# A table loaded in two transfers instead of four, thirteen matmuls ahead of a small network, two constants set by another engine

## The chip, the cores and the metric

The kernel runs on one core of a Trainium2 chip. The metric is the device time of one execution in microseconds (us), as the median over several runs; lower is better. Beside the timed runs there is one profiled execution, whose trace is quoted below.

## The reference, cut to what matters

Attention over 4 batches, 8 heads, 576 positions and 64 dimensions, with a bias that a small network makes from the distance of two positions; then a mixing step of low rank and a two-layer MLP over the 512-wide result.

```python
scores = scale * np.matmul(q, k.transpose(0, 1, 3, 2))
psi_rel = np.log1p(np.abs(pos[:, None] - pos[None, :]))
psi_i = np.log1p(np.maximum(pos[:, None], 1.0))
h = np.maximum((psi_rel / psi_i)[..., None] @ w1 + b1, 0.0)    # 32 hidden units
scores = scores + (h @ w2).transpose(2, 0, 1)[None]
attn = np.exp(scores - scores.max(-1)) / (sum + 1e-09)
x = heads of np.matmul(attn, v), side by side
u = x + (x.transpose(0, 2, 1) @ U @ V).transpose(0, 2, 1)
out = u + np.maximum(u @ w_ch1, 0.0) @ w_ch2
```

## The kernel before

The program is one long list per engine, written out by hand; each engine runs its list in order and waits at semaphores. SyncE (SP) and ScalarE (ACT) issue the DMAs, each on a queue of its own. The kernel has three stages: the bias network (about the first 65 us), the 16 pairs of heads of the attention, and the MLP. The change touches only the start of the first.

**The network.** Positions go in 36 groups of 16 rows (T = 32 to 35 first, then 0 to 31). For each T there are four hidden tiles (cg = 0 to 3), each 128 partitions (4 rows of positions times 32 hidden units) by up to 576 distances: `relu(table + psi)`, where the table is log1p of the distance times w1 and psi is one number per partition. `bias_hid` (L299) makes them: cg 0 by ACT (L308), cg 1 to 3 by VectorE (DVE, L310). `bias_mm` (L320) multiplies them by w2 on TensorE (PE, L328): the four cg use four column groups of 32 and run beside each other. `bias_out` (L339) scales the result from PSUM into SBUF by ACT (L342), and SP stores it to DRAM (L345), from where it is loaded again, row by row shifted, as the bias of the scores. ACT alternates between L308 of a later T and L342 of an earlier one. Between them stand the first steps of the attention: ACT casts q and k of the first pair (`raw`) into `hi` (L182) and DVE takes the difference (L192).

**What comes before the network.** `head` in DRAM is 128 x 641: column 0 is w1, and columns 1 on are the table for four subs of 32 rows each, of which sub s is read from column 1 + s on. Four loads fetch it into `tab` (L284), two issued by SP (subs 0, 1) and two by ACT (subs 2, 3). SP then issues w1 (L285, 128 rows of 4 bytes), `ident` (L781) and the two halves of `raw` (L154); ACT issues `small` (L286: b1, psi, w2 and scales, 128 rows of 852 bytes), then loads its function table and runs a first `warm` instruction (L289). DVE multiplies the table by w1 (L293), then psi by b1 (L294), then sets two constants (L782 `sgn`, L783 `eps`), and starts on the hidden tiles. GpSimd (POOL) clears two strips at the start (L276, L278) and has nothing else to do until L798.

Of the kernel before, what the change touches and what calls it, by code (L numbers as in the profile page):

```python
# [9 lines left out]
F32 = mybir.dt.float32  # L10
# [9 lines left out]
B, H, S, D = 4, 8, 576, 64  # L20
HP = H // 2
DM = H * D
# [3 lines left out]
HID = 32  # L26
P = 128
# [5 lines left out]
LINE = 16  # L33
NTAB = 2 * S - 1
CUT = 640
# [10 lines left out]
ALL_DVE = (6, 12, 16, 19, 24)  # L46

CW = 256

KD = DM // P  # L50
WQ = KD * DM
# [10 lines left out]
def kernel(  # L62
# [14 lines left out]
    nc = tc.nc  # L77
    mm = nc.tensor.matmul
# [14 lines left out]
    def psum(tag, shape, name):  # L93
        rot[tag].append(rot[tag].pop(0))
        pl = rot[tag][-1]
        return pl.tile(shape, F32, tag="a" if pl is psA else tag, name=name)
# [22 lines left out]
    sgn = const.tile([P, 1], I32, name="sgn")  # L119

    eps = const.tile([P, 9], F32, name="eps")[:, 0:1]
# [4 lines left out]
    x_sb = mix.tile([P, 5, DM], F32, name="x_sb")  # L126
# [24 lines left out]
    def load_part(p, a, e):  # L151
        b, hp = divmod(p, HP)
        for lo in (0, D):
            nc.sync.dma_start(out=raw[lo : lo + D, a:e], in_=qk[b, hp, :, a:e])  # L154
# [76 lines left out]
    def conv_ops(src, n, finish):  # L231
        st = {}

        def load():
            st["raw"] = wrawp.tile([P, CW], I64, tag="wraw", name="wraw")
            nc.sync.dma_start(out=st["raw"][:, 0:n], in_=src)
            words = st["raw"].bitcast(I32).rearrange("p (n t) -> p n t", t=2)
            st["l"], st["h"] = words[:, 0:n, 0], words[:, 0:n, 1]

        def size():  # L240
            st["t"] = wcp.tile([P, CW], I32, tag="t", name="wt")[:, 0:n]
            st["y"] = wyp.tile([P, CW], I32, tag="wy", name="wy")[:, 0:n]
            nc.scalar.activation(out=st["t"].bitcast(F32), in_=st["h"].bitcast(F32), func=AF.Abs)
# [32 lines left out]
    nc.gpsimd.memset(e5[:, NE:], 0.0)  # L276
    e_all = ring[1][:, 3 * S : 3 * S + 5 * (S + LINE)].rearrange("p (i y) -> p i y", i=5)
    nc.gpsimd.memset(e_all[:, :, NE : S + LINE], 0.0)  # L278
    e_ring = [e_all[:, i, :] for i in range(5)] + [e5]
    w1_sb, tab = wtab[:, S : S + 1], wtab[:, 0:S]  # L280
    small_sb = tabp.tile([P, SMALL], F32, name="small_sb")
    for sub in range(4):
        rows = slice(sub * HID, (sub + 1) * HID)
        (nc.sync, nc.scalar)[sub // 2].dma_start(out=tab[rows], in_=head[rows, 1 + sub : 1 + sub + S])  # L284
    nc.sync.dma_start(out=w1_sb, in_=head[:, 0:1])  # L285
    nc.scalar.dma_start(out=small_sb, in_=small)  # L286
    warm = tabp.tile([P, 1], F32, name="warm")
    nc.vector.memset(warm, 0.0)
    nc.scalar.activation(out=warm, in_=warm, func=AF.Relu)  # L289

    b1_sb, psi_sb = small_sb[:, 0:1], small_sb[:, 1 : 1 + S // 4]
# [466 lines left out]
    def weight_jobs(g, fin):  # L758
        jobs = []
        for which in range(2):  # L760
            for k in range(KD):
                for a in range(0, DM, CW):
                    if which == 0:
                        src = w_ch1[k * P : (k + 1) * P, g * DM + a : g * DM + a + CW]
                    else:
                        r = (g * FG + k) * P
                        src = w_ch2[r : r + P, a : a + CW]
                    jobs.append((src, CW, fin(g, which, k, a, a + CW)))
# [10 lines left out]

    pools["pt"] = p1.enter_context(tc.tile_pool(name="ptp", bufs=1, side="left"))  # L780
    nc.sync.dma_start(out=ident, in_=ident_in)  # L781
    nc.vector.memset(sgn.bitcast(F32), -2.0)  # L782
    nc.vector.memset(eps, 1.0e-9)  # L783
    load_part(0, 0, QKW)
    new_pair(0)
    order = [32, 33, 34, 35] + list(range(32))
# [5 lines left out]
    for i in range(len(order) + 2):  # L792
# [4 lines left out]
        if i == len(order) - 1:  # L797
            nc.gpsimd.tensor_scalar(  # L798
                out=warm, in0=hids[order[i]][3][:, 0:1], scalar1=1.0, scalar2=0.0, op0=ALU.mult, op1=ALU.add
# [24 lines left out]
    for c, hp in ((4, 1), (3, 0), (0, 1)):  # L824
# [6 lines left out]
        out=rep[:, 0 : 3 * RANK].rearrange("p (g r) -> p g r", g=3),  # L831
# [5 lines left out]
        out=rep[:, 3 * RANK : P], in0=fold[:, 0:RANK], in1=fold[:, 0:RANK], op=ALU.subtract  # L837
# [28 lines left out]
    for p in range(NP):  # L866
# [6 lines left out]
        for s in range(9):  # L873
# [27 lines left out]
            if p == NP - 3 and s == 1:  # L901
                t = big.tile([P, 9 * S], F32R, tag="big0", name="w1q")
# [3 lines left out]
            if p == NP - 2 and s == 1:  # L906
                t = big.tile([P, 9 * S], F32R, tag="big1", name="w2q")
# [5 lines left out]
            if p == NP - 1 and s == 1:  # L913
                t = big.tile([P, 9 * S], F32, tag="big2", name="acc")
# [65 lines left out]
    t = big.tile([P, 9 * S], F32R, tag="big3", name="ut")  # L980
    h1, h3, l3 = big_views(t, [(2 * UT, KD)] * 2 + [(UT, 2)])
    utq = t
    t = [qkp.tile([P, K0 + 2 * LINE], F32R, tag="lo", name="ut") for _ in range(2)]
# [67 lines left out]
    def turns(j):  # L1051
        return [lambda a=a, i=i: make_ut(a, i) for a in (j, j + 1) for i in range(TT)] if j < NB else [lambda: None] * 4
# [158 lines left out]
    t = turns(3)  # L1211
# [173 lines left out]
    for q in range(NQ):  # L1385
# [6 lines left out]
        segs, c = layer1(q)  # L1392
# [3 lines left out]
        first, pend = pend[:2], pend[2:]  # L1396
# [12 lines left out]
    for n, q in enumerate(order2):  # L1409
# [4 lines left out]
        one, c = layer1(q)  # L1414
# [84 lines left out]
```

## Time and profile before

| | |
|---|---|
| time, median of 3 runs | 729.49 us (728.93 to 730.12) |
| time of the profiled execution | 727.51 us |
| its span, first to last instruction | 725.7 us |
| TensorE busy in the span | 707.5 us (97%) |
| VectorE, ScalarE, GpSimd busy | 537.1, 402.9, 273.1 us |
| DMA traffic | 127.19 MB, mean 175 GB/s |
| granted TensorE clock, mean | 1.000 |

The span runs from the first to the last instruction; the profiled execution's own time is 1.8 us more than its span. It is 2.0 us under the median of the three timed runs, so a change in time is worked out against the profiled execution and then put on the median. Busy time of TensorE counts pipelined matmuls that overlap; at the start of the program TensorE waits for data, and how long is read from the first microseconds of the trace.

### The profile page before, as it was taken

Reading aid. Unit: us, or ns where it says so; the run is one execution under the profiler, and the core shown is the slowest. Engines: PE = TensorE matmul, PEld = TensorE weight load, DVE = VectorE, ACT = ScalarE, POOL = GpSimd, SP = SyncE. Lnnn points to the kernel's source line nnn. Section 1 sums busy time; section 2 is a strip of 40 time slices with the busy share of each in tenths; the row PEclk is TensorE's granted clock in tenths of the full one; section 3 lists DMA queues with packets and bytes.
Section 4 is the critical chain, followed back from the end, with each engine's and each line's share of the span. In section 5 each row is a group of like instructions: output and inputs, shape, how many; then the busy total and the mean of one; then the engine's idle time right before and its main releaser. Section 6 shows DMA issues by size and latency. Waiting matters only on the chain.

```text
span 725.7 us, 13129 instructions
## 1 busy us (share of the span) xinstructions
PE 707.5 (97%) x4620; PEld 561.2 (77%) x4620; DVE 537.1 (74%) x1202; ACT 402.9 (56%) x915; POOL 273.1 (38%) x287
## 2 busy tenths in 40 slices
PE   6999999999999999999999999999999999999997
PEld 2547888788777877878787888888787788888886
DVE  7985688788787777656658689999999953655545
ACT  7897778788778778864223335555555421222220
POOL 0006967567655557701150323536436300000000
PEclk9999999999999999999999999999999999999999
DMA  6889984565565546522293504637434665633313
GB/s 204 272 312 294 304 230 117 140 184 159 140 176 156 144 122 183 182 97 88 74 355 128 206 29 153 217 135 275 149 117 160 239 259 180 256 125 122 155 58 117
DMA packets 53393, 127.19 MB, mean 175 GB/s; under 512 B 8784, under 2 KB 12368, under 8 KB 52048
## 3 DMA queue, kind: packets, MB, share of 16 engines
q1 hardware_dynamic: 53088, 126.10, 53.1%
q8 instruction: 37, 0.61, 0.4%
q10 hardware_dynamic: 240, 0.26, 0.1%
q14 instruction: 28, 0.23, 0.1%
HBM read 81.34 MB, written 44.99 MB: 174 GB/s over the span
## 4 chain that ended last, share of the span: by engine, by line
PE 74%; ACT 9%; DVE 9%; issue 3%; DMA 2%; POOL 2%; SPq 0%; DVEq 0%; POOLq 0%; ACTq 0%
PE po L1334 15%; PE sb L1273 12%; PE o L508 11%; PE sc L399 10%; PE ph L676 7%; PE tb L472 7%; PE po L701 5%; PE bs L328 2%; ACT p L425 1%; POOL wy L266 1%; DVE acc L1320 1%; ACT pt L452 1%; ACT ring L308 1%; PE ph L1362 1%; ACT ring L342 1%
## 5 line engine op out<-in xcount | busy, mean ns | idle before, releaser
L1320 DVE TENSOR_TENSOR acc<-po,acc 128x512 f32<-128x512 f32 x108 | 74.1, 687 | 50.5 <-PE po L1334 44.1
L425 ACT ACTIVATE p<-p,st 128x576 f32<-128x576 f32 x128 | 99.9, 781 | 11.0 <-DVE st L407 10.6
L407 DVE CUSTOM_DVE_ANT_0 p<-sc,bias 128x576 f32<-128x576 f32 x128 | 95.9, 751 | 9.2 <-DMA bias<-bias_dram 4.7
L266 POOL TENSOR_TENSOR wy<-wt,wy 128x256 int32<-128x256 int32 (+1 forms) x68 | 50.3, 740 | 135.4 <-DVE wt L261 118.4
L399 PE MATMUL sc<-hi 128*128 128x288 f32 x320 | 100.6, 331 | 0.1
L399 PE MATMUL sc<-lo,hi 128*128 128x288 f32 x320 | 89.1, 295 | 0.0
L508 PE MATMUL o<-pt,v 128*64 128x320 f32 (+1 forms) x640 | 85.4, 411 | 0.1
L472 PE MATMUL tb<-ident,p 128*128 128x128 f32 x512 | 78.3, 275 | 1.4 <-DVE pt L454 0.9
L1334 PE MATMUL po<-wq,hq 128*128 128x512 f32 x288 | 73.5, 391 | 0.5 <-DVE ut L1367 0.5
L399 PEld LDWEIGHTS sc<-hi 128*128 128x128 f32 x320 | 60.3, 189 | 11.5 <-issue 8.0
L472 PEld LDWEIGHTS tb<-ident,p 128*128 128x128 f32 x512 | 59.8, 140 | 10.9 <-issue 7.6
L508 PEld LDWEIGHTS o<-pt,v 128*64 128x64 f32 x640 | 44.4, 136 | 30.1 <-issue 3.0
L452 ACT COPY pt<-tb 128x512 f32<-128x512 f32 x88 | 51.3, 582 | 23.4 <-PE tb L472 23.2
L1334 PEld LDWEIGHTS po<-wq,hq 128*128 128x128 f32 x288 | 53.5, 188 | 12.6 <-DVE ut L1367 0.9
L399 PEld LDWEIGHTS sc<-lo,hi 128*128 128x128 f32 x320 | 60.6, 189 | 0.5
L1273 PE MATMUL sb<-ut,w1q 128*128 128x512 f32 x216 | 55.1, 390 | 0.4 <-ACT acc L1277 0.3
L1273 PE MATMUL sb<-ut,wq 128*128 128x512 f32 x216 | 55.0, 390 | 0.5 <-ACT acc L1277 0.4
L328 PE MATMUL bs<-ring,small_sb 128*32 128x512 f32 (+48 forms) x640 | 43.8, 400 | 9.2 <-ACT ring L308 6.7
L701 PE MATMUL po<-w2q,hh 128*128 128x512 f32 x216 | 52.2, 393 | 0.4 <-DVE x_sb L576 0.4
L1334 PE MATMUL po<-w2q,ut 128*128 128x512 f32 x180 | 49.1, 389 | 0.0
L676 PE MATMUL ph<-ut,w1q 128*128 128x512 f32 (+1 forms) x240 | 48.2, 351 | 0.5 <-DVE ut L646 0.5
L1277 ACT COPY acc<-sb 128x512 f32<-128x512 f32 x48 | 28.0, 583 | 36.5 <-PE sb L1273 36.3
(153 smaller groups left out, 1447.6 us busy)
## 6 DMA issues: line engine op xcount, KB each, us to landing
wraw<-in_w_ch_dram SPq DMA_DIRECT2D x64, 256.0 KB, 3.4
raw<-in_qk_dram SPq DMA_DIRECT2D x50, 304.0 KB, 4.1
bias_dram<-ring SPq DMA_DIRECT2D x30, 296.0 KB, 3.9
acc<-u_dram SPq DMA_DIRECT2D x26, 256.0 KB, 4.6
ub_dram<-ut SPq DMA_DIRECT2D x12, 512.0 KB, 4.7
w_dram<-wq SPq DMA_DIRECT2D x12, 512.0 KB, 4.5
ut<-ub_dram SPq DMA_DIRECT2D x12, 512.0 KB, 4.3
v<-in_vp_dram SPq DMA_DIRECT2D x16, 320.0 KB, 3.0
```

What stands on the lines that cost most here:

```text
L328: mm(bs[T][32 * cg : 32 * cg + 32, o + a : o + e], lhsT=w2_sb, rhs=hid[:, far + left - e : far + left - a][:, ::-1] if a >= left else hid[ ...
L399: mm(ps[:, a, 0:HALF], lhsT=hi[:, q0 : q0 + P], rhs=kk, start=(i == 0), stop=(i == n - 1))
L407: nc.vector.tensor_tensor_reduce(out=halves(d["dst"]), in0=d["ps"][:, :, 0:HALF], in1=halves(bias[hp][:, s * S : (s + 1) * S]), scale=-0.1 ...
L425: nc.scalar.activation(out=dst, in_=dst, func=AF.Exp, bias=st[:, s : s + 1], scale=-1.0, accum_out=st[:, 10 + s : 11 + s])
L452: nc.scalar.copy(out=out, in_=in_)
L472: nc.tensor.transpose(bank[:, kb, :], src[:, b0 + kb * P : b0 + (kb + 1) * P], ident)
L508: mm(o[hd * D : (hd + 1) * D, 0:n], lhsT=v[:, vb * D : (vb + 1) * D], rhs=pt[:, pb, :], start=(j == 0), stop=(j == 4),)
L676: mm(st["ps"][:, f, :], lhsT=w, rhs=x, start=(i == 0), stop=(i == 3 * KD - 1))
L701: mm(ps, lhsT=h, rhs=w, start=(m == 0), stop=(m == 3 * nf - 1))
L1273: mm(bank[b], lhsT=w[:, c, r, :], rhs=u[:, r, :], start=first and i == 0, stop=i == 5, skip_group_check=True)
L1320: nc.vector.tensor_tensor(out=a, in0=ps, in1=a, op=ALU.add)
L1334: mm(ps, lhsT=h, rhs=w[:, r, :], start=m == 0, stop=m == 5)
```

## The change

The four loads of the table become two, one per queue, each of two subs: `flat` is `head` as one row of numbers, cut into two blocks of one sub each (`s`), and each block into 32 rows (`r`) of 576 numbers. The number 13 of `WARM` is how many matmuls of 128 x 128 zeros go to TensorE ahead of the network, into a PSUM tile that nobody reads; VectorE clears the 128 columns of `x_sb` they read. GpSimd sets `sgn` and `eps` at the start, where VectorE did it between L294 and the first hidden tile.

```diff
+WARM = 13
...
+    nc.gpsimd.memset(sgn.bitcast(F32), -2.0)
+    nc.gpsimd.memset(eps, 1.0e-9)
...
-    for sub in range(4):
-        rows = slice(sub * HID, (sub + 1) * HID)
-        (nc.sync, nc.scalar)[sub // 2].dma_start(out=tab[rows], in_=head[rows, 1 + sub : 1 + sub + S])
+    row, step = CUT + 1, HID * (CUT + 1) + 1
+    flat = head.rearrange("p c -> (p c)")
+    for i, (eng, o) in enumerate(((nc.sync, 0), (nc.scalar, LINE))):
+        two_subs = flat[2 * i * step - o : 2 * (i + 1) * step - o].rearrange("(s x) -> s x", s=2)
+        eng.dma_start(
+            out=tab[2 * i * HID : 2 * (i + 1) * HID],
+            in_=two_subs[:, 0 : HID * row].rearrange("s (r c) -> s r c", c=row)[:, :, 1 + o : 1 + o + S],
+        )
     nc.sync.dma_start(out=w1_sb, in_=head[:, 0:1])
     nc.scalar.dma_start(out=small_sb, in_=small)
     warm = tabp.tile([P, 1], F32, name="warm")
     nc.vector.memset(warm, 0.0)
+    nc.vector.memset(x_sb[:, 0, 0:P], 0.0)
+    first = psum("t", [P, DM], "first")
+    for _ in range(WARM):
+        mm(first[:, 0:P], lhsT=x_sb[:, 0, 0:P], rhs=x_sb[:, 0, 0:P], start=True, stop=True)
     nc.scalar.activation(out=warm, in_=warm, func=AF.Relu)
...
     nc.sync.dma_start(out=ident, in_=ident_in)
-    nc.vector.memset(sgn.bitcast(F32), -2.0)
-    nc.vector.memset(eps, 1.0e-9)
```

In the lists below a name such as DMAHW0 is one of eight semaphores that the DMAs take in turn. SP's list at the start of the program, before:

```order
L284 DMA wtab<-in_head_dram 32x576 x2
L285 DMA wtab<-in_head_dram 128x1
L781 DMA ident<-in_ident_dram 128x128
L154 DMA raw<-in_qk_dram 64x2432
L154 DMA raw<-in_qk_dram 64x2432 [waits DMAHW0_49]
L345 DMA bias_dram<-ring 128x592 [waits DMAHW1_49,Activation_49,Pool_49]
```

The same place of SP's list with the change:

```order
L290 DMA wtab<-in_head_dram 64x1x576
L294 DMA wtab<-in_head_dram 128x1
L794 DMA ident<-in_ident_dram 128x128
L156 DMA raw<-in_qk_dram 64x2432 x2
L358 DMA bias_dram<-ring 128x592 [waits Activation_49,Pool_49]
L358 DMA bias_dram<-ring 128x592 [waits DMAHW0_49,Activation_49]
```

Every load behind the table moves up by one issue, and the second half of `raw` waits for nothing now. ACT's list changes in the same way: one table load, then `small`.

VectorE's list at the same place, before (`wtab` holds the table and w1):

```order
L288 MEMSET warm 128x1
L293 TENSOR_SCALAR wtab<-wtab 128x576 [waits DMAHW3_49,DMAHW2_49,DMAHW5_49,DMAHW1_49,DMAHW0_49]
L294 TENSOR_SCALAR small_sb<-small_sb 128x144 [waits DMAHW4_49]
L782 MEMSET sgn 128x1
L783 MEMSET eps 128x1
L310 TENSOR_SCALAR ring<-wtab,small_sb 128x528 [waits DVE_49]
```

The same place with the change:

```order
L297 MEMSET warm 128x1
L298 MEMSET x_sb 128x128
L306 TENSOR_SCALAR wtab<-wtab 128x576 [waits DMAHW3_49,DMAHW1_49,DMAHW0_49]
L307 TENSOR_SCALAR small_sb<-small_sb 128x144 [waits DMAHW2_49]
L323 TENSOR_SCALAR ring<-wtab,small_sb 128x528 [waits DVE_49]
```

The multiplication of the table still waits for every load of the table and for w1; the two constants are gone from behind L294, and one memset stands ahead of the wait.

TensorE's list with the change; before, it began with the row of L328 that is L341 here:

```order
L301 MATMUL first<-x_sb 128x128 [waits DVE_49]
L301 MATMUL first<-x_sb 128x128 x12
L341 MATMUL bs<-ring,small_sb 32x512 [waits DMAHW2_49,Activation_49]
L341 MATMUL bs<-ring,small_sb 32x512 [waits DVE_49] x3
L341 MATMUL bs<-ring,small_sb 32x15 x4
```

The thirteen stand ahead of the network's first matmul and wait only for the memset; nothing behind them moved.

## Rows read from the trace of the kernel before

**Rows 1.** The page's busy times, share of the span and instructions.

```profile
PE 707.5 (97%) x4620; PEld 561.2 (77%) x4620; DVE 537.1 (74%) x1202; ACT 402.9 (56%) x915; POOL 273.1 (38%) x287
```

**Rows 2.** The chain of waits, first 9 us: start us, us, what.

```profile
0.74 0.39 SPq L284
...
1.19 0.41 SPq L284
...
1.65 2.28 DMA wtab<-in_head_dram
...
4.05 0.52 DVE wtab L293
4.57 0.21 DVE small_sb L294
...
4.78 0.04 DVE eps L783
4.82 0.74 ACT ring L308
...
5.60 2.82 PE bs L328 x18
...
8.44 0.75 ACT ring L342
```

**Rows 3.** Timeline, first 30 us, one merged row of VectorE: start, us, what.

```profile
4.81 12.45 DVE L310 TENSOR_SCALAR ring<-wtab,small_sb 128x528 f32<-128x528 f32 x30
```

**Rows 4.** Busy us of each engine from 8.5 to 17 us, clock, DMA.

```profile
core 0: us, PE busy (x) PEld busy (x) DVE busy (x) ACT busy (x) POOL busy (x), PEclk, DMA share, GB/s
8.50:17.00 8.50, 8.37 (x184) 3.29 (x176) 8.50 (x22) 8.50 (x14) 0.00 (x0) 1.00 0.61 218
```

**Rows 5.** Groups of VectorE, first 20 us: busy us, mean ns, idle before.

```profile
L192 DVE TENSOR_TENSOR hi<-raw,hi 64x1216 fp32r<-64x1216 f32 x1 | 1.4, 1422 | 0.8 <-ACT hi L182 0.8
```

**Rows 6.** DMA view, 0 to 12 us: 40 slices' GB/s; issues, KB each, us to landing.

```profile
GB/s 0 0 0 0 0 31 261 285 192 241 240 267 39 401 324 454 65 422 97 130 259 97 357 97 357 130 389 162 97 292 32 0 0 95 363 371 182 47 402 387
...
wtab<-in_head_dram ACTq DMA_DIRECT2D x2, 72.0 KB, 2.4
wtab<-in_head_dram SPq DMA_DIRECT2D x2, 72.0 KB, 2.2
small_sb<-in_small_dram ACTq DMA_DIRECT2D x1, 106.5 KB, 2.4
...
wtab<-in_head_dram SPq DMA_DIRECT2D x1, 0.5 KB, 2.3
```

**Rows 7.** DMA queue, 9.9 to 12 us (stores of 2,368-byte rows): packets, MB, engines' share.

```profile
q1 hardware_dynamic: 243, 0.54, 66.3%
```

**Rows 8.** The page's DMA queue over the whole span: packets, MB, engines' share.

```profile
q1 hardware_dynamic: 53088, 126.10, 53.1%
```

**Rows 9.** DMA queue, 3.6 to 6 us (the loads of raw): packets, MB, engines' share.

```profile
q1 hardware_dynamic: 96, 0.58, 95.4%
```

**Rows 10.** Groups of TensorE, 5 to 6.5 us, then 10 to 12 us: busy us, mean ns.

```profile
L328 PE MATMUL bs<-ring,small_sb 128*32 128x512 f32 x6 | 1.9, 1061 | 5.6 <-ACT ring L308 5.6
...
L328 PE MATMUL bs<-ring,small_sb 128*32 128x512 f32 x20 | 2.8, 593 | 0.0
```

**Rows 11.** The page's costliest groups: xcount, busy us, mean ns.

```profile
L508 PE MATMUL o<-pt,v 128*64 128x320 f32 (+1 forms) x640 | 85.4, 411 | 0.1
```

**Rows 12.** The chain of waits near 74 us: a 128 x 128 pass pair.

```profile
73.87 0.22 PE tx L526 x2
```

**Rows 13.** Busy us of each engine in the last 4 us, columns as in rows 4.

```profile
722.00:724.00 2.00, 0.02 (x1) 0.00 (x0) 0.69 (x1) 0.00 (x0) 0.00 (x0) 1.00 0.55 204
724.00:725.70 1.70, 0.00 (x0) 0.00 (x0) 0.00 (x0) 0.00 (x0) 0.00 (x0) 0.85 0.19 69
```

**Rows 14.** Waits of GpSimd, first 60 us: total us, times, longest.

```profile
POOL warm L798 <- ACT ring L308: 54.5, 1, 54.5
```

## The prediction

> **What bounds the kernel now.** I read the page's busy times first: TensorE is busy for 97% of the span [rows 1], so a gain or a loss counts only where TensorE, or what it waits for, stands still. The change touches the first 5 us alone, so the second view is the chain of waits there [rows 2]. It says that everything hangs on the loads: SP issues two table loads (0.74 and 1.19) and w1 as its third DMA (1.65), w1 has landed at 3.93, DVE multiplies table and psi (4.05 to 4.78), ACT and DVE make the first hidden tiles (4.82), TensorE starts at 5.60, and at 8.44 ACT takes the first group's result. From 4.81 to 17.26 DVE makes 30 hidden tiles without a gap, one each 0.415 us [rows 3], and from 8.5 to 17 ACT is busy for the whole 8.5 us [rows 4]. The only slack of DVE is 0.8 us ahead of L192, where it waits for ACT's cast of `hi` [rows 5]. So a delay of the table passes one to one into both engines, and from there into stores, bias loads and scores, which all wait in a row for these two; what comes earlier at ACT alone is worth at most what DVE can follow. Nothing in this stage is tied to a fixed time, so I let a shift that stands at L192 stand at the end.
>
> **The change part by part.**
>
> *Two constants and the memsets.* In the chain the two constants cost DVE 0.04 us between L294 and the first tile [rows 2]; that is what leaves. POOL has nothing to do for 54.5 us after its start [rows 14], so two memsets more cost nothing there; SP's first store, which waits for POOL, stands behind ACT's result of 8.44 anyway. The memset of 128 columns on DVE lies in DVE's wait for the table. I count 0.
>
> *The issues.* Each load on SP's queue takes about 0.4 us to issue and the next begins 0.45 us after the one before [rows 2]. With one table load per queue, w1 is issued at 1.19 instead of 1.65 and `small` as much earlier; `ident` and `raw` too. If the table itself lands no later, that is a gain of 0.46 us: w1 was the last of what DVE waited for.
>
> *The table's transfer.* This is the term that decides. Before, a table load has 32 rows as the outermost count on both sides, and the slices from 1.8 us on show 192 to 285 GB/s [rows 6], so many DMA engines work on them. In the new form the source begins with a count of 2 (two subs), then 32 rows; the destination begins with 64. No load of this kernel begins with less than 32, so no row shows how such a load is divided, and I bound it. One end: its 64 rows go over all 16 engines as before. Other end: it is cut where both sides can be cut alike at the outermost count, into 2, one sub per engine. Then both queues' loads sit on two engines, each of which moves 64 rows of 2,304 bytes, 147 KB. What one engine moves: 0.54 MB in 66.3% of 16 engines' 2.1 us is 24.2 bytes per ns for rows of nearly this size [rows 7]; over the whole run 20.5 [rows 8]; beside the loads of `raw`, which the other engines now work on at the same time, 15.8 [rows 9]. That is 6.1, 7.2 or 9.3 us. I take 22 bytes per ns, between the first two, since rows of the same size are nearest and `raw` slows a part of it: 6.7 us. The fixed part of a landing is 2.2 us less the 0.4 us in which 16 engines move two such loads (9.2 KB each at 24.2): 1.8 us [rows 6]. So the table lands at 0.74 + 1.8 + 6.7 = 9.24 instead of the 3.93 at which DVE was released, **5.3 us later**; `small` follows the table on ACT's queue and is covered by the 0.4 us in which DVE multiplies the table.
>
> I take this narrow end, because an even division of counts of 2 and 64 has no more than two parts, and nothing in the written load offers the 64 source rows as one count: the step between the subs (32 x 641 + 1) is not 32 times the step of a row.
>
> The Trainium skill states the same as a rule: by "DMA: Bandwidth & Descriptors", section "Why a DMA increments its semaphore by 16 and not by 1", a DMA is divided along the slowest dimension above 1 of either side, over the largest number of engines up to 16 that divides both. By that rule the four old loads run on 16 engines, which the 192 to 285 GB/s agree with, and the two new ones on 2; with it the sum is 5.3 us slower, without it (16 engines) 1.2 us faster, as worked out under the rivals. No run here has shown a load with a count of 2.
>
> *Thirteen matmuls.* A full-precision matmul is two passes: 320 calls of L508 stand as 640 [rows 11]. Two 128-column passes at the higher clock take 0.22 us in the chain [rows 12], so thirteen take 2.9 us there and about 5.7 us at half the clock. They begin at about 1.1 us, after the memset, and end between 4.0 and 6.8 us; TensorE had stood still until 5.60, so they are covered as long as the network's first matmul is ready later than that. What they can give: the first 512-wide passes last 1,061 ns, those after 10 us 593 [rows 10], so TensorE began at the lower of its two levels (1.2 GHz) and changed to the higher (2.4) near 8.4 us, although the clock column reads 1.00 throughout. With the table at 9.24 the first matmul comes at 5.60 + 5.3 = 10.9, 4 to 7 us after the thirteen have ended. At the end of the run the granted clock is 1.00 until 724 us and 0.85 in the last 1.7 us, so it fell at about 725.2, 3.2 us after the last matmul (722.0) [rows 13]. A wait of 4 to 7 us is longer, so I expect the network to start at the lower level as before, and count 0. If the level holds, it is worth up to 0.8 us here, DVE's slack [rows 5].
>
> **Sum** against the profiled execution: 727.51 + 5.3 = 732.8 us. The three timed runs have a median 1.98 us above it, so I forecast 729.49 + 5.3 = **734.8 us**, 0.7% slower. About 0.2% (1.46 us) is what a measurement of this kernel can tell from no change.
>
> **The rivals.**
>
> *1. The rows go over the 16 engines after all (ends not slower).* Place: the two loads at 0.74. Then w1, issued 0.46 us earlier, releases DVE at about 3.6; the thirteen matmuls end about when the network's first is ready (5.1), at the higher level. The last of the first group's tiles is ready at about 5.7, and its two 512-wide passes save 2 x 0.47 us [rows 10], so ACT starts 1.4 us earlier; DVE can follow by 0.46 + 0.8 [rows 5]. Gain 1.2 us: 728.3 us, inside 0.2%, unless TensorE's slow start is longer in the timed runs than in the profiled one, which their higher median would allow. For it: all rows are of one size and one column step, and every load seen was spread. Against it: the count of 2. It decides from about ten engines on: 295 KB at 22 bytes per ns land by 3.93 only if the transfer takes 1.4 us.
>
> *2. The same, but the clock rises late.* With the table early and TensorE at the lower level throughout, the thirteen hold it until 6.8, where the network was ready at 5.1. Its hidden tiles then wait, and the first group needs some 2.3 us of the 2.82: ACT starts near 9.1 instead of 8.44. About 0.6 us lost: 730.1 us, no change that can be told. It decides if the level rises after about 6 us.
>
> *3. Two engines, and the rest queues up behind them.* `raw` and the first stores have their share on the same two engines, behind the table. By 15.8 bytes per ns [rows 9] the table takes 9.3 us and DVE starts 7.9 us later: 737.4 us. For it: `raw` is issued 1 us after the table. Against it: its rows lie on the other engines' time too, and half of the table goes to other partitions.
>
> **How the numbers follow.** Forecast 0.76; rival 1 0.13; rival 2 0.06; rival 3 0.05. The forecast's own range goes from 24.2 bytes per ns with the 0.8 us of the clock (+3.9 us, 733.4), with some 0.4 us less in the fixed part, to half-way to rival 3 (+7.3): 733.0 to 736.8. To leave out no more than 2 in 10 the range has to take in rivals 1 and 2 below it: **728.3 to 736.8**. Rival 1 ends past 0.2% in about a third of its cases: faster 0.05. The rest of it and rival 2, with a few cases in which the loads are slow and most of it is hidden: same 0.15. Slower 0.80.
>
> **What would show it.** Right: the table's loads land some 8.5 us after their issue instead of 2.2; the slices from 3 to 8 us hold long rows on few engines; the multiplication of the table starts near 9.4 and is the end of DVE's longest wait; the thirteen run from 1.1 and end by 6.8; the network's first 512-wide passes, near 10.9, again last 1,061 ns; the chain's first stretch is the table's DMA; L192 and the first store come 5 us later, and the rest of the trace is the old one moved. Wrong: table loads that land within 3 us, and ACT's first result before 8.4. If the loads are slow but the end is not, then some wait in the first 60 us has slack that I did not see, and the bias loads before the first scores are where to look.

## The result: 1.0% slower, and the profile after

The changed kernel takes 736.74 us (median of 4 runs, 736.65 to 736.97) against 729.58 us for the kernel before (4 runs beside it). The ratio is 1.0104, with a 95% interval of 1.0091 to 1.0117: 7 us slower. The forecast was 734.8; the value lies at the upper end of the range, and by the ratio to the median from which the forecast starts (729.49 x 1.0104 = 737.1) 0.3 us beyond it. The direction and the place were right, the size was not. The profiled execution of the changed kernel took 736.67 us, 9.2 more than that of before (727.51).

The chain of waits of the changed kernel, its first 20 us (start us, us, what), answers to [rows 2] (the same lines of code have numbers 2 to 13 higher here):

```profile
0.74 0.71 SPq L290
1.45 0.06 issue
1.51 11.85 DMA wtab<-in_head_dram
...
13.48 0.52 DVE wtab L306
14.01 0.22 DVE small_sb L307
...
14.25 0.74 ACT ring L321
...
15.03 4.52 PE bs L341 x38
...
19.58 0.75 ACT ring L355
```

The DMA that releases DVE is w1's, issued at 1.51 right behind SP's table load. It is in the chain for 11.85 us where it was 2.28. DVE multiplies the table at 13.48 instead of 4.05: **9.43 us later, where I had put 5.3**. TensorE starts at 15.03 instead of 5.60, which is the same 9.43. The last row is ACT's second result; its first comes at 17.88 instead of the 8.44 of [rows 2], again 9.4 later.

The DMA view of the changed kernel from 0 to 12 us (GB/s in 40 slices; then issues with KB each and us to landing) answers to [rows 6]. For the table's two loads this view gives no time to landing:

```profile
GB/s 0 0 0 0 0 0 0 23 8 47 186 316 116 370 136 378 347 290 96 275 193 113 323 80 258 242 160 307 63 242 225 48 18 26 18 21 45 55 44 49
...
raw<-in_qk_dram SPq DMA_DIRECT2D x2, 608.0 KB, 14.0
wtab<-in_head_dram SPq DMA_DIRECT2D x1, 144.0 KB
wtab<-in_head_dram ACTq DMA_DIRECT2D x1, 144.0 KB
small_sb<-in_small_dram ACTq DMA_DIRECT2D x1, 106.5 KB, 10.4
...
wtab<-in_head_dram SPq DMA_DIRECT2D x1, 0.5 KB, 11.8
```

Every load of the start lands late, even w1 with 4 bytes a row and `small`: each has its share on the engines at which the table is queued. The list of packets in the trace shows it: of `small`'s 128 rows, which is 8 for each of 16 engines, 112 are done by 3.7 us, and the other 16, two engines' share, come between 9.7 and 11.8. Of the 128 rows of `raw` 112 have begun by 9.5, and 16 come from 12.3 on.

The busy times by stretch of the changed kernel (columns as in [rows 4]) show the thirteen matmuls and the clock:

```profile
1.00:5.40 4.40, 4.32 (x20) 4.32 (x21) 0.03 (x1) 1.49 (x2) 0.00 (x0) 1.00 0.58 151
5.40:6.30 0.90, 0.89 (x8) 0.70 (x7) 0.00 (x0) 0.00 (x0) 0.00 (x0) 1.00 0.98 188
6.30:8.80 2.50, 0.00 (x0) 0.00 (x0) 0.00 (x0) 0.00 (x0) 0.00 (x0) 1.00 0.98 193
8.80:15.00 6.20, 0.00 (x0) 0.00 (x0) 1.48 (x4) 0.75 (x2) 0.00 (x0) 0.50 0.24 53
15.00:19.00 4.00, 3.97 (x32) 2.37 (x36) 4.00 (x11) 2.39 (x4) 0.00 (x0) 0.50 0.06 17
19.00:22.00 3.00, 3.00 (x92) 1.83 (x84) 2.84 (x7) 2.72 (x5) 0.00 (x0) 0.99 0.55 204
```

TensorE is busy from 1.08 to 6.3 (20 passes in 4.4 us, then 8 in 0.9, so its level rose near 5.4, although the column reads 1.00 from the start) and still until 15.0; the granted clock is 0.50 (1.2 GHz) from 8.8 until 19, then 1.00 (2.4 GHz). So the level that the matmuls had reached was gone when the network came, as forecast. The groups of TensorE by form, 15 to 18.5 us and 20 to 22 us (columns as in [rows 10]), say the same in durations:

```profile
L341 PE MATMUL bs<-ring,small_sb 128*32 128x512 f32 x16 | 4.3, 1042 | 8.7 <-ACT ring L321 8.7
...
L341 PE MATMUL bs<-ring,small_sb 128*32 128x512 f32 x20 | 2.8, 594 | 0.0
```

From there on the trace is the old one moved. DVE's hidden tiles again run without a gap up to L194 (timeline of VectorE; [rows 3, 5]):

```profile
14.25 5.09 DVE L323 TENSOR_SCALAR ring<-wtab,small_sb 128x528 f32<-128x528 f32 x12
19.50 7.44 DVE L323 TENSOR_SCALAR ring<-wtab,small_sb 128x576 f32<-128x576 f32 x18 [0.16 <-PE bs L341]
27.86 1.42 DVE L194 TENSOR_TENSOR hi<-raw,hi 64x1216 fp32r<-64x1216 f32 x1 [0.92 <-ACT hi L184]
```

L194 starts at 27.86 instead of 18.03 (+9.8), and the last instruction ends 9.1 us later than before (spans 734.9 and 725.7).

### The profile page after: what moved, and what is told of

It is laid out like the page before. It is cut to its first block, busy times and chain, and to the rows that moved or that the text cites. A ratio compares the mean times of both kernels' runs of the same rounds, so it can differ in the third digit from the quotient of the medians.

```text
span 734.9 us, 13179 instructions
## 1 busy us (share of the span) xinstructions
PE 712.9 (97%) x4646; PEld 566.6 (77%) x4646; DVE 538.7 (73%) x1201; ACT 402.7 (55%) x915; POOL 272.3 (37%) x289
## 4 chain that ended last, share of the span: by engine, by line
PE 68%; DVE 13%; ACT 8%; DMA 4%; POOL 4%; issue 3%; SPq 0%; DVEq 0%; POOLq 0%; ACTq 0%
PE po L1345 12%; PE o L521 11%; PE sc L412 11%; PE sb L1284 9%; PE tb L485 7%; PE ph L689 5%; PE po L714 4%; PE bs L341 4%; POOL wy L268 2%; DVE acc L1331 2%; DMA wtab<-in_head_dram 2%; DVE wt L263 2%; DVE acc L1291 1%; DMA u_dram<-acc 1%; ACT p L438 1%
## 5 line engine op out<-in xcount | busy, mean ns | idle before, releaser
L438 ACT ACTIVATE p<-p,st 128x576 f32<-128x576 f32 x128 | 100.0, 782 | 10.8 <-DVE st L420 10.4
L341 PE MATMUL bs<-ring,small_sb 128*32 128x512 f32 (+48 forms) x640 | 44.1, 404 | 12.0 <-ACT ring L321 9.9
```

Source lines behind the costliest of these rows:

```text
L341: mm(bs[T][32 * cg : 32 * cg + 32, o + a : o + e], lhsT=w2_sb, rhs=hid[:, far + left - e : far + left - a][:, ::-1] if a >= left else hid[ ...
L438: nc.scalar.activation(out=dst, in_=dst, func=AF.Exp, bias=st[:, s : s + 1], scale=-1.0, accum_out=st[:, 10 + s : 11 + s])
```

## The experiments

Eleven kernels ran in twelve experiments, one of them twice (2 and 5). The theory: two engines carry the table, and DVE's late start is the whole loss. The rivals: the matmuls or the constants cost something; something else slows the loads; the loss is not passed on one to one. Ratios are to the kernel before, run beside each.

**1. The four old loads in the changed kernel.**

```diff
-    for i, (eng, o) in enumerate(((nc.sync, 0), (nc.scalar, LINE))):
...
+    for sub in range(4):
+        rows = slice(sub * HID, (sub + 1) * HID)
+        (nc.sync, nc.scalar)[sub // 2].dma_start(out=tab[rows], in_=head[rows, 1 + sub : 1 + sub + S])
```

> The changed kernel with the four old table loads; the thirteen matmuls and GpSimd's constants stay. Theory (the whole loss is the transfer of the two table loads): DVE's first multiplication starts near 4.0 us again, as in the kernel before. The thirteen matmuls end near 6.3 us (they ran from 1.08 to 6.29 in the changed kernel), so the network's first matmul waits from 5.6 to 6.3, but runs at the higher level; its first group then takes about 1.5 us instead of 2.82 and ACT starts near 7.8 instead of 8.44. Time: 0.6 us under the kernel before, 729.0, within what can be told from no change. Rival (the matmuls cost by themselves): TensorE ends the first group later than 8.44 and the time is above the kernel before by 0.6 us or more. Rival (something else of the change costs, not the loads): 733 us or more.

727.37 us (12 runs, 726.34 to 729.61), ratio 0.998 [0.9968, 0.9991]. The loss is gone, so it is all in the two loads; and the rest of the change gains 0.2% (by the ratio 1.5 us, where I had expected 0.6 below before). Its chain:

```profile
1.08 5.91 PE first L296 x26
6.99 1.33 PE bs L336 x24
...
8.35 0.75 ACT ring L350
```

DVE started at 4.44, not quite the 4.0 expected. The matmuls ended at 6.99, later than the 6.3 expected (the level rose at about 7.1 in this execution), but the network then ran its first group in 1.33 us instead of 2.82, so ACT started at 8.35 against 8.44.

**2. The two loads alone, in the kernel before.** Its edit is the loop of the two loads from the change, and nothing else.

> The kernel before with nothing but the two table loads in place of the four. Theory: all of the loss is here; the table's last piece lands at 13.1 us, DVE starts near 13.5, and the time is 736 to 738 us, as in the changed kernel. In the changed kernel TensorE fell back to the lower level before the network began, so without the thirteen matmuls nothing is lost. Rival (the matmuls or the constants are part of the loss): 733 to 735 us.

743.67 us (4 runs, 738.11 to 744.08), ratio 1.0182 [1.0151, 1.0213]. That they cost the whole loss holds; that they cost no more than the changed kernel does not. DVE started at 13.42 and the network at 14.97, both as in the changed kernel, so the difference arises later (5 and 12).

**3. The loads of `raw` after the table.**

```diff
+    gate = tabp.tile([P, 1], F32, name="gate")
+    nc.sync.dma_start(out=gate, in_=w1_sb)
     load_part(0, 0, QKW)
```

> The changed kernel with one small load more on SP's queue (128 rows of 4 bytes out of w1's column) ahead of the loads of raw: it waits for w1, which is the last on the two engines, so raw comes after the table. Theory (the loads of raw on the other engines halve the rate of the two): the table's packets keep their 93 to 100 ns, the 64 of each engine take 6.1 us from 2.2, and the table lands at 8.5 to 9.5 us; DVE starts near 9.5 instead of 13.48 and the time falls by about 4 us, to 732 to 733. Rival (two queues that share an engine halve its rate): the packets still take about 200 ns while both queues run, DVE starts after 12.5, and the time stays at 736 to 737.

734.3 us (4 runs), ratio 1.007 [1.0049, 1.0091], against 1.0104 for the changed kernel; 732 to 733 was expected. DVE starts at 10.11 instead of 13.48, somewhat later than the 9.5 expected, so 3.4 of the 9.4 us came from `raw` (the chain):

```profile
1.51 8.47 DMA wtab<-in_head_dram
...
10.11 0.52 DVE wtab L306
```

The DMA view of this kernel, 5 to 7.5 us, the count of packets under a size, then queues (packets, MB, share of 16 engines):

```profile
DMA packets 55, 0.13 MB, mean 51 GB/s; under 512 B 0, under 2 KB 0, under 8 KB 55
...
q10 hardware_dynamic: 28, 0.06, 6.6%
q1 hardware_dynamic: 27, 0.06, 6.3%
```

and the same view of the changed kernel, 5 to 10.4 us:

```profile
DMA packets 168, 0.94 MB, mean 174 GB/s; under 512 B 29, under 2 KB 32, under 8 KB 84
...
q1 hardware_dynamic: 140, 0.88, 84.2%
q10 hardware_dynamic: 28, 0.06, 6.2%
```

Without `raw`, 12.9% of 16 engines are busy: that is 2.06 engines, and they move 55 rows of 2,304 bytes in 2.5 us, 25 bytes per ns each. With `raw` beside them, 84 - 32 = 52 such rows take 5.4 us: 11.1 bytes per ns each, less than half. The other engines are slow then too. From 5 to 9 us `raw` is under way throughout, in the changed kernel beside the table and in the kernel before alone:

```profile
DMA packets 131, 0.84 MB, mean 210 GB/s; under 512 B 14, under 2 KB 14, under 8 KB 54
```

```profile
DMA packets 106, 0.87 MB, mean 216 GB/s; under 512 B 17, under 2 KB 17, under 8 KB 17
```

That is 13.1 and 13.5 bytes per ns for each of 16 engines; the two with the table have 11.5 (54 - 14 = 40 rows in 4 us). So the total is nearly the same with the table as without, and while `raw` runs every engine is slow, not only these two. What holds them there, no run here shows. The rival (two queues on one engine halve its rate) falls: in the kernel with `raw` after the table both queues run on the two engines all the while.

**4. One count of 64.** The rows of each sub lie in memory already moved by sub columns.

```diff
-        two_subs = flat[2 * i * step - o : 2 * (i + 1) * step - o].rearrange("(s x) -> s x", s=2)
...
+        rows = slice(2 * i * HID, 2 * (i + 1) * HID)
+        eng.dma_start(out=tab[rows], in_=head[rows, 1 : 1 + S])
```

> The changed kernel, but the table lies in memory with each sub's rows already moved by sub columns (a matter of layout), so that each of the two loads has 64 rows as its one count; two loads, two queues, thirteen matmuls as in the changed kernel. Theory (the count of 2 sets two engines; 64 rows go over 16): the two loads land by 3 us, w1 by 3.5, DVE starts near 3.6 instead of 13.48; TensorE is still busy with the thirteen until 6.3 and ACT starts near 7.8. Time 728.5 to 729.2, about 7.5 us under the changed kernel. Rival (it is two loads instead of four as such, with half as many queues' entries, that is slow): DVE starts after 8 us and the time is 733 or more.

728.29 us (12 runs), ratio 0.9989 [0.9978, 1.0]. Two loads of the same bytes on the same two queues (DMA view, 0 to 12 us):

```profile
wtab<-in_head_dram SPq DMA_DIRECT2D x1, 144.0 KB, 2.9
wtab<-in_head_dram ACTq DMA_DIRECT2D x1, 144.0 KB, 3.4
```

The queues of the same kernel from 2.5 to 3 us, when nearly all packets are the table's (packets, MB, share of 16 engines):

```profile
q10 hardware_dynamic: 41, 0.09, 53.8%
q1 hardware_dynamic: 49, 0.08, 41.1%
```

So it is not two loads instead of four, it is the count of 2 that the source begins with. By the Trainium skill (DMA: Bandwidth & Descriptors, section "Why a DMA increments its semaphore by 16 and not by 1") a DMA runs on the largest number of engines up to 16 that divides the slowest count above 1 of both its sides: 2 for 2 and 64, 16 for 64 and 64. The trace agrees with both: 2.06 busy engines in experiment 3, and 94.9% of 16, or 15.2, here. No run has another small count. The table of 64-row loads lands somewhat later than the 2.2 to 2.4 us of the four [rows 6], and w1 behind it; DVE started at 4.44 (3.6 was expected), as with the four loads of experiment 1, so saving two issues gained nothing either.

**5. The two loads alone, a second look.** The kernel of experiment 2.

> The kernel before with the two loads alone, a second time, because three of its four runs took 743.7 us and only the profiled one 738.1: the thirteen matmuls seem to give back 7 us that I had counted as nothing. Theory (clock): in the longer execution TensorE stays at the lower level (512-wide passes of 1,061 ns) for well over the 4.4 us of the first look, so the stage up to 45 us itself is longer. Rival (transfers): the stage up to 40 us is as in the first look, and the 5.6 us are DMA waits in the chain later, at the bias loads before the scores. If the profile shows 738 again, the question stays open.

739.75 us in its one run. The network stage is as in the first look (start 15.10, passes of 1,061 ns, the clock up near 20 us). DVE waited longer for bias loads between 40 and 125 us; in the groups of VectorE there, the same row of the changed kernel and of this one (idle before, and what ended it):

```profile
L420 DVE CUSTOM_DVE_ANT_0 p<-sc,bias 128x576 f32<-128x576 f32 x32 | 24.0, 753 | 8.2 <-PE sc L412 4.2 <-DMA bias<-bias_dram 3.8
```

```profile
L412 DVE CUSTOM_DVE_ANT_0 p<-sc,bias 128x576 f32<-128x576 f32 x32 | 24.0, 753 | 9.6 <-DMA bias<-bias_dram 6.3 <-PE sc L404 3.1
```

That speaks for the rival (transfers) as far as 739.75 goes. The 743.7 us were not in a profile, so their cause stays open.

**6. Fifty matmuls**, to hold the clock until the network comes.

```diff
-WARM = 13
+WARM = 50
```

> The changed kernel with fifty matmuls over the cleared tile instead of thirteen. The first thirteen end at 6.3 us as before; 37 more at 0.22 us each take 8.1, so they end near 14.5, just ahead of the network's first matmul at 15.03, which then begins at the higher level. Theory (the clock's second fall costs what the low passes of the changed kernel took, and DVE can follow by 0.8 us): the first passes last 593 ns, ACT's first result comes at 17.5 to 18 instead of 19.58, and the time falls by 0.8 to 2 us, to 734.7 to 736. Rival (the time of TensorE there is hidden behind DVE and ACT): 736.5 to 737.

740.25 us (4 runs, 738.78 to 741.61), ratio 1.0164 [1.0144, 1.0183]: slower than thirteen, against both expectations. The clock did hold, and the first passes were short (groups by form, 15 to 17 us):

```profile
L341 PE MATMUL bs<-ring,small_sb 128*32 128x512 f32 x15 | 2.5, 605 | 0.8 <-ACT ring L321 0.8
```

ACT's first result came at 16.91 us instead of 17.88, and its second, which is the 19.58 of the expectation, at 18.22, 1.36 us earlier than in the changed kernel. By 55 us 0.37 of that was left, and at 75 us the kernel lay 0.5 us behind it, in part because the bias loads came later: DVE waited 4.8 us for them where the changed kernel waited 3.8 (the row that experiment 5 shows of the changed kernel, in this one):

```profile
L420 DVE CUSTOM_DVE_ANT_0 p<-sc,bias 128x576 f32<-128x576 f32 x32 | 24.0, 753 | 9.7 <-DMA bias<-bias_dram 4.8 <-PE sc L412 4.0 <-PE tb L485 0.8
```

So what the faster network gained at 15 to 20 us was given back among the stores and loads from 40 us on. By the end another 1.9 us were lost, which no row here places.

**7. Four loads and ten matmuls.** The edit is that of experiment 1 with `WARM = 10`.

> The four old loads, GpSimd's constants and ten matmuls instead of thirteen. With thirteen TensorE was still at them until 6.99 us where the network was ready at about 5.9, since the level rose at 7.10 only. Ten at the lower level end 1.3 us earlier, at 5.6, and the network follows without a pause. Theory (the last three were in the way): ACT's first result comes at 7.3 to 8.2 and the time is 0 to 0.8 us below the 727.37 of four loads with thirteen. Rival (a shorter run of matmuls lets the level rise later): the first group takes over 2.5 us and the time goes back towards the 729.25 of the kernel before.

727.49 us (11 runs), ratio 0.998 [0.997, 0.9989], the same as with thirteen. ACT started at 8.03 instead of 8.35 (the ten ended at 5.72), which the end does not show.

**8. Four loads and no matmuls**, so GpSimd's constants alone.

> The four old loads and GpSimd's constants without any matmul ahead of the network, so the constants' move (and DVE's memset of 128 columns) alone. Theory (constants are worth nothing, the matmuls gave the 1.9 us of four loads with thirteen): 729.0 to 729.5, as the kernel before. Rival (the constants gave it): 727.4.

729.04 us (12 runs), ratio 1.0001 [0.999, 1.0013]. The constants are worth nothing, as forecast; the 1.7 us between this and experiment 1 (1.5 by the ratios) are the matmuls'.

**9. w1 in the table's rows.** Four loads, nine matmuls.

```diff
-        (nc.sync, nc.scalar)[sub // 2].dma_start(out=tab[rows], in_=head[rows, 1 + sub : 1 + sub + S])
-    nc.sync.dma_start(out=w1_sb, in_=head[:, 0:1])
+        (nc.sync, nc.scalar)[sub // 2].dma_start(out=wtab[rows, 0 : S + 1], in_=head[rows, 0 : S + 1])
```

> Four loads on 16 engines as before, but the table lies in memory with its rows already moved and with w1 as the last column, so that w1's own load of 128 rows of 4 bytes is gone; nine matmuls; constants by GpSimd. In the four-load kernels DVE started at 4.39 to 4.44, released by w1, whose last piece came at 4.3, while the table had landed by 3.1. Theory (w1 alone held DVE): DVE starts at 3.2 to 3.7, the network at 4.9 to 5.3, right behind the nine matmuls, and the time is 0.3 to 0.9 us below the 727.4 of four loads with ten or thirteen. Rival (the later stages set the time, not the start): 727.4 again.

727.98 us (12 runs), ratio 0.9977 [0.9966, 0.9987]: no better than experiments 1 and 7. The time that the theory forecast did not come; DVE started at 3.94, later than the 3.2 to 3.7 expected, and then psi waited for `small` (the chain):

```profile
1.65 3.26 DMA small_sb<-in_small_dram
...
4.94 0.31 DVE small_sb L301
...
6.05 4.20 PE bs L335 x20
```

The nine matmuls ended at 5.29, TensorE stood still until 6.05, and its clock rose only near 10.2.

**10 and 11. All loads early, DVE held**, with thirteen matmuls and with none.

```diff
     nc.vector.memset(x_sb[:, 0, 0:P], 0.0)
+    for _ in range(6):
+        nc.vector.memset(x_sb[:, 1:5], 0.0)
```

> Four loads, thirteen matmuls, and DVE held by six memsets of a tile that nothing reads yet, so that it multiplies the table at some 12 to 14 us, as late as in the changed kernel, while all loads come early. Theory (the loss is the late start of DVE and nothing else of the slow loads): a start of 12 to 14 us costs what it costs in the changed kernel (7.2 us for a start that is 9.4 later), so 735 to 738 us. Rival (the slow loads cost more than the start, since raw and the bias stores queue behind them): under 734.

> The same late start of DVE with four loads, but without the matmuls. Two loads alone gave 738 to 744 us, in runs that scatter, and the changed kernel 736.7 in all runs. Theory (without the thirteen, TensorE's slow first groups move the stores onto the bias loads, and what is lost there depends on small shifts): 738 to 744, scattering as with two loads alone. Rival (it was the two loads that scattered): 735 to 738, as with thirteen.

739.14 us (737.51 to 740.0), ratio 1.0124 [1.0104, 1.0144], and 739.71 us (738.92 to 741.54), ratio 1.0138 [1.0118, 1.0159]. In both DVE multiplied the table at 14.38 (the chain of experiment 10 counts it from the end of the last memset, 14.46):

```profile
12.70 1.76 DVE x_sb L295
14.46 0.31 DVE wtab L303
14.78 0.21 DVE small_sb L304
```

A start that is 10.3 us late costs 9.0 us by the ratio with the matmuls and 10.1 without, although here no load is slow (the table's land in 2.3 to 2.5 us in experiment 10). So the late start by itself makes the loss. The time with thirteen lies above the 735 to 738 expected, since the start came later than in the changed kernel. Without them the runs reach 741.5, not the 744 of experiment 2. They scatter as much with the thirteen (737.5 to 740.0) as without, and the two intervals overlap, so the theory of experiment 11 is not borne out and its rival not excluded.

**12. Two loads and the constants, no matmuls.** The changed kernel with its loop of matmuls taken out.

> The changed kernel without its matmuls: two loads and GpSimd's constants. Theory (the matmuls make the difference between 736.7 and two loads alone): 738 to 744. Rival (the constants do): 736.5 to 737.

739.2 us (738.26 to 743.08), ratio 1.0138 [1.0112, 1.0164]. As the theory has it, without the matmuls the time is above 736.74; how much varies between runs.

How a late start is passed on, in the profiled executions, against that of before (us):

| kernel (experiment) | DVE's table | ACT's second result | DVE's eighth sum of scores and bias (64.7 us before) | end |
|---|---|---|---|---|
| raw after the table (3) | +6.06 | +6.72 | +6.43 | +6.58 |
| changed kernel | +9.44 | +9.82 | +9.25 | +9.14 |
| two loads alone (2) | +9.37 | +9.96 | +10.53 | +10.58 |
| two loads alone (5) | +9.50 | +10.15 | +11.42 | +12.24 |
| fifty matmuls (6) | +9.47 | +8.46 | +9.77 | +11.54 |
| DVE held, thirteen (10) | +10.33 | +10.75 | +10.14 | +9.98 |
| DVE held, none (11) | +10.33 | +10.20 | +11.07 | +11.57 |
| two loads, constants (12) | +9.71 | +10.26 | +10.53 | +11.21 |

The start is passed on one to one, within -0.4 and +2.7 us. What varies is lost or gained at the stores and loads of the bias and near the end. It does not follow the clock of the first groups: the three kernels with thirteen matmuls, which begin at the lower level, end -0.4 to +0.5 us from their start, and the one with fifty, at the higher, +2.1. The four without matmuls end +1.2 to +2.7. Why thirteen lose least is not shown.

## Why the prediction was wrong in size

**The table on two engines: right.** The source's count of 2 set it (experiments 3 and 4), the transfer stood in the chain, DVE, the network and L194 moved with it. 16 engines (rival 1) did not come true for this form; experiment 4 shows what they would have given.

**What one engine moves: here the forecast failed.** "I take 22 bytes per ns, between the first two, since rows of the same size are nearest and `raw` slows a part of it." Alone the two engines moved 25, a little better than that. But `raw` was under way for about 6 of the 10 us of the transfer, and beside it they moved 11.1, below even the 15.8 [rows 9] that I kept as the far end. Rival 3 had that end, and I gave it 0.05 with the argument that `raw`'s rows "lie on the other engines' time". 112 of its 128 rows did lie there, and the two engines lost more than half of their rate all the same. So [rows 9] should have been read as a price for whatever runs beside `raw`, not for engines that carry it; and the same view from 5 to 9 us, 216 GB/s, would have given 13.5. At 13.5 my sum comes to 9.5 us, which is near the 9.43 in part by luck, since the rate was 25 and 11.1 by turns. Of the 9.4 us, 3.4 are `raw`'s (experiment 3). The remaining 6.06 are 0.8 above my 5.3. In that stretch w1 comes behind the table on the same two engines, `small`'s share runs between its rows, and the load takes longer to issue (0.71 against 0.39 us [rows 2]); how the 0.8 divides was not measured.

**From the start to the end: right, with an error on the other side.** "I let a shift that stands at L192 stand at the end": in the profiles +9.83 at that place (27.86 against 18.03) became +9.14 at the end. But I then added 1.98 us because the timed runs of before lie above their profiled one. The changed kernel's runs do not lie above theirs (736.65 to 736.97 against 736.67). So 9.2 us between the profiled executions show as 7.2 between the medians, and this made the forecast look nearer than its term was: 727.51 + 5.3 is 3.9 us under the 736.67 of the changed kernel's own profile. The upper end of the range has a slip too: half-way between my 5.3 and rival 3's 7.9 is 6.6 us, not 7.3.

**Thirteen matmuls: right in the profile, not in the sum.** They ran from 1.08 to 6.29, covered; the network began at the lower level, as I had it from the 3.2 us at the end of the run [rows 13] (here the clock fell 2.5 us after the last of them). In the profiles the network stage is the same with and without them, yet the kernels with two loads and without them take 739.2 to 743.7 us (medians) against 736.74. I had counted 0. Experiments 10 and 11 give 0.6 us for the same matmuls, which their intervals do not tell from nothing; the difference arises behind 40 us, and its cause stays open.

**Constants, memsets, issues: right for the first two** (experiment 8: 1.0001). The issues' 0.46 us never showed: in the changed kernel w1 was issued at 1.51, not 1.19, since the longer load takes 0.71 us to issue, and even with 64 rows as one count DVE started at 4.44. In the kernels with four loads (1, 7, 8) it started at 4.39 to 4.44, where the kernel before has 4.05; there w1 took 2.62 us instead of 2.28 (experiment 8), for a reason that was not looked for.

Of the marks that I named, the table's last row ended 11.9 us after its issue (12.6 in the trace) where I had the landing 8.5 us after it, the multiplication at 13.48 instead of 9.4, the first 512-wide passes at 15.03 instead of 10.9; the places were those named.

The best version is the change without its two loads: four loads, ten or thirteen matmuls, 0.2% faster than the kernel before (ratio 0.998 in both, the intervals below 1; experiment 9 cannot be told from them) and about 9 us faster than the changed kernel.

## What to carry to other kernels

Before merging loads, look at the count with which either side of the new pattern begins: the same bytes in a pattern that begins with 2 came 9 us later than with 64. When a transfer is on few engines, price it at the rate that the trace shows while the neighbouring traffic runs, not at the rate of an engine alone, and add what is queued behind it on those engines. Start the sum and end it in the same execution: the distance between a profiled run and the median of before need not hold for the kernel after.

## What was not expected of the hardware

- Two engines fell from 25 to 11.1 bytes per ns each beside a load that ran on the others, while all 16 together moved 210 GB/s from 5 to 9 us, almost the 216 that the same load moves alone. The cause was not found.
- A granted clock that holds through the network's start (experiment 6) brought ACT's second result forward by 1.4 us, and the kernel still ended later. Here, where the stage ends in stores and loads, an earlier producer was no gain by itself.
- With the same thirteen matmuls from 1.08 us on, TensorE's level rose near 5.4 us in the changed kernel and near 7.1 in experiment 1, so the time of the rise differs between profiled executions.
